# Seven more bias row sets on VectorE, and another order where the second expert layer begins

## The chip, the cores and the metric

The kernel runs on one core of a Trainium2 chip. A core has TensorE (matrix products, PE in the profile; its weight loads are PEld), VectorE (DVE), ScalarE (ACT), GpSimd (POOL) and SyncE (SP), whose queue issues nearly all transfers here. The metric is the device time of one execution in microseconds, the median of several executions; less is better.

## The reference

Three layers follow one another, all in float32, for 4 batches of 576 positions: attention with 8 heads of 64 and a learned position bias, a gated layer of width 512, and a layer that turns its input by learned angles, mixes positions, and then channels.

```python
x = (psi_rel / psi_i)[..., None]              # 576 x 576, from log1p of distances
bias = np.maximum(x @ w1 + b1, 0.0) @ w2      # 32 hidden, 8 heads
attn = softmax(q @ k.T / 8 + bias) @ v
# first expert layer: x = attn, transposed to 4 x 576 x 512
gate = 1.0 / (1.0 + np.exp(-causal_conv5(x, conv_w)))
x = (gate * (x @ w_val)) @ w_out
# second expert layer
theta = x @ w_theta
zr, zi = x * np.cos(theta), x * np.sin(theta)
y = w_tok_r @ zr + w_tok_i @ zi               # over positions
u = x + y
out = u + np.maximum(u @ w_ch, 0.0)
```

## The kernel before

**The bias stage** (the first 57 us) makes the 576 x 576 x 8 bias in 36 groups of 16 rows. For a group four tiles `h`, here called row sets, are made from the table `wpsi`: each is a maximum with a per-partition number, 304 to 577 wide. A set marked `d` is made by VectorE (line 158), one marked `a` by ScalarE (line 160). The pattern of a group is `ddda`, or `dddd` for the groups listed in `cfg["D4"]`. TensorE multiplies the sets with the second weights (line 171) into the tile `bp`, of which there are two; ScalarE scales them out of it into `ev` (line 181), and a transfer writes them to a table `scr`, from where they come back as `bias`. The order within this stage is set by the tile scheduler, which also threads the first steps of attention into it (`cfg["S0"]`).

**Attention** works in units of 128 rows and two heads: scores `s` by TensorE (line 236, two halves of 288 columns), then on VectorE line 250, which adds the bias and takes the row's extreme value (called the soft step here), the exponential on ScalarE (line 253), the normalization on GpSimd (line 265), transposes and products with the values. There are two score tiles, `s0` and `s1`, used in turn, and three tiles `ns` between VectorE and ScalarE. From the end of the bias stage on the order is the one that the code is written in.

**The products of the expert layers** are made in three matmuls each (`mm3`, lines 108 to 110): every operand is split into an upper word, a rounded copy made by ScalarE, and a lower word, the difference of both, made by GpSimd, or by VectorE where a table says `d` (`split`, lines 63 to 65). The lower word waits for the upper one.

**The second expert layer begins** in `m2`, in written order; each engine takes its instructions in that order. For batch 0 and position block t, `theta(0, t)` is 12 matmuls of 512 columns; `turns` (ScalarE, line 626) and `fold` (VectorE, line 631) reduce the angle; `trig` is three ScalarE steps (lines 637 to 639); `x(0, t)` transposes the input block on TensorE (line 645) into one of two tiles `xk_p`, so that x(0, 2) waits for the reader of x(0, 0), and so on; `z(0, t)` multiplies it on VectorE by cosine and sine (line 652, two instructions) and splits the first half of both into the upper and lower words `za`, index 0 for the cosine and 1 for the sine. Block t = 4 is a tail shared by two batches; `m2_ztail` and `m2_z8` make it. The channel weights come as 64-bit numbers, in four blocks: `L` loads one, `A` (ScalarE) and `D` (VectorE, lines 989 to 991) turn it to float32, `H` splits it, with the upper word on ScalarE (line 995) and the lower word on GpSimd (line 997). `m2_sums(0, 0)` makes the sums' words, later parts more of them (lines 666 to 680). Then `m2_tok` runs the mixing products p1, p2, p4, p6, p7, p5, p3 on TensorE; their result tiles `pp` are three, so that p6 waits until VectorE has added p1 (line 742). p1 reads the four cosine blocks of `za`, p2 the sine blocks and the tail, p4 `zb` of the sums, p6 the words that line 675 makes.

Of the kernel before, what the change touches and what calls it, by code (L numbers as in the profile page):

```python
# [14 lines left out]
PSUM = bass.MemoryType.PSUM  # L15
# [21 lines left out]

cfg = dict(

    D4=(14, 16, 18, 20, 22),  # L40

    HB=5, VB=10,

# [9 lines left out]

    TH=(0,),

    CLO='pppp', ZLO={}, SLO='p',
    XLO={(0, 4): 'p', (1, 0): 'p', (1, 1): 'p'},
)

# [53 lines left out]
class Kernel:  # L113
# [702 lines left out]
    def m2(self, top, mm, pool, T):  # L816


        tc = self.tc
        theta, turns, fold, trig, x, z = (self.m2_theta_mm, self.m2_turns, self.m2_fold, self.m2_trig, self.m2_x,  # L820
                                          self.m2_z)
        raw = self.zb_p.tile([128, KC, DM, 2], I32, tag="zb", name="raw_ch")
        blocks = [self.chan_block(raw, kc) for kc in range(KC)]

        def chan(*todo):
            for f in todo:
                blocks[int(f[1])][f[0]]()

        self.m2_fetch(1, 0)
        chan('L0', 'L1', 'A1')  # L830
        self.xk_p = pool(mm, "n_xk", 2, space=PSUM, **T)
        chan('L3', 'L2')
        self.m2_load(0)
        turns(0, 0)
        fold(0, 0)
        self.m2_fetch(0, 4)
        theta(0, 1)
        chan('A0')
        self.m2_fetch(1, 1)
        trig(0, 0)  # L840
        turns(0, 1)
        self.m2_split(0, 4)
        chan('D0')
        theta(0, 2)
        x(0, 0)
        turns(0, 2)
        self.m2_split(1, 0)
        fold(0, 1)
        trig(0, 1)
        z(0, 0)  # L850
        chan('H0')
        self.m2_split(1, 1)
        chan('A2')
        fold(0, 2)
        chan('D1')
        theta(0, 3)
        turns(0, 3)
        trig(0, 2)
        x(0, 1)
        x(0, 2)  # L860
        z(0, 1)
        x(0, 3)
        fold(0, 3)
        chan('H1', 'A3', 'D2')
        trig(0, 3)
        theta(0, 4)
        turns(0, 4)
        z(0, 2)
        fold(0, 4)
        chan('D3')  # L870
        self.m2_load(1)
        theta(1, 0)
        chan('H2')
        trig(0, 4)
        chan('H3')
        turns(1, 0)
        x(0, 4)
        z(0, 3)
        theta(1, 1)
        turns(1, 1)  # L880
        self.m2_ztail(0)
        self.m2_z8(0)
        zb = self.zb_p.tile([128, 2, 2, 4, 256], F32R, tag="zb", name="zb")
        for i, slots in enumerate((self.zh, self.zl)):
            slots += [zb[:, i, k] for k in range(2)]
        fold(1, 0)
        self.m2_sums(0, 0)
        trig(1, 0)
        fold(1, 1)
        mm.close()  # L890
        self.pp = pool(top, "n_pp", 3, space=PSUM, **T)
        self.xk_p = pool(top, "n_mm", 2, space=PSUM, **T)
        for b in range(B):
            for i, _ in enumerate(self.m2_tok(b)):
                if b == 0:
                    if i == 0:
                        self.m2_sums(0, 1)
                        self.m2_sums(0, 2)
                    if i == 1:
                        trig(1, 1)  # L900
                        self.m2_sums(0, 3)
                    if i == 2:
                        self.m2_sums(0, 4)
                    if i == 3:
                        self.m2_fetch(1, 2)
                        self.m2_fetch(1, 3)
                    if i in (5, 6):
                        self.m2_split(1, i - 3)
                elif i == 0:
                    self.m2_sums(b, 3)  # L910
                elif i == 1:
                    self.m2_sums(b, 4)
            ts = {0: (2, 3), B - 1: ()}.get(b, (0, 1, 2, 3))
            line, prev = [], None

            def turn():
                nonlocal prev
                cur = line.pop(0) if line else None
                if cur:
                    turns(*cur)  # L920
                if prev:
                    trig(*prev)
                if cur:
                    fold(*cur)
                prev = cur

            for t in ts:
                theta(b + 1, t)
                turn()
                line.append((b + 1, t))  # L930
                if b == 1 and t == 1:
                    self.m2_prep(2, 4)
            if b == 1:
                theta(2, 4)
                turn()
                line.append((2, 4))
            at = {0: 0, 1: 1, 2: 2, 4: 3}
            for i in range(2 * KC):
                n, m = i // KC, i % KC
                if b + 1 < B and i in at:  # L940
                    x(b + 1, at[i])
                if b == 1 and i == 3:
                    x(2, 4)
                if m % 2 == 0 and i:
                    out = self.pc
                self.m2_chan(b, n, m)
                if m % 2 == 0 and i:
                    new, self.pc = self.pc, out
                    self.m2_out(b, (i - 2) // KC, (i - 2) % KC)
                    self.pc = new  # L950
                if b + 1 < B and i in at:
                    z(b + 1, at[i])
                turn()
                if b == 1 and i == 3:
                    self.m2_ztail(2)
                if b + 1 < B and i == 5:
                    self.m2_sums(b + 1, 0)
                    self.m2_sums(b + 1, 1)
                if b + 1 < B and i == 6:
                    self.m2_sums(b + 1, 2)  # L960
                    self.m2_z8(b + 1)
                if b + 2 < B and i < 4:
                    self.m2_prep(b + 2, i)
            self.m2_out(b, 1, 2)
            if b + 2 < B:
                self.m2_load(b + 2)
# [8 lines left out]
    def chan_block(self, raw, kc):  # L975
# [17 lines left out]
        def parts():  # L993
            x, hi, lo = h.bitcast(F32), self.wv[0][:, kc], self.wv[1][:, kc]
            nc.scalar.activation(out=hi, in_=x, func=AF.Copy)
            eng = nc.gpsimd if cfg["CLO"][kc] == "p" else nc.vector
            eng.tensor_tensor(out=lo, in0=x, in1=hi.bitcast(F32), op=ALU.subtract)
# [79 lines left out]
    def run(self):  # L1077
# [12 lines left out]
        with ExitStack() as top:  # L1090
# [16 lines left out]
            with ExitStack() as att:  # L1107
# [12 lines left out]
                with ExitStack() as bs:  # L1120
# [19 lines left out]
                    for n in range(NG):  # L1140
                        q = "dddd" if n in cfg["D4"] else "ddda"
                        pend.append((n, q, self.bias_group(n, q, hp, pp)))
# [205 lines left out]
```

## Time and profile before

| what | us |
|---|---|
| median of 3 runs | 606.78 |
| lowest and highest | 606.68, 610.57 |
| the profiled execution | 611.05 |
| its span, first to last instruction | 609.3 |
| mean granted TensorE clock | 0.990 of full |

The profile is of one execution, whose time lies 1.75 us above its span and 4.27 us above the median. Rows of the timeline give start and length in us, engine, line, operation, `out<-in` by tile names, shapes, and how many instructions a row stands for; in brackets stands the idle time of the engine ahead of it, and what ended it.

### The profile page before, as it was taken

How to read it: one execution, taken by the hardware profiler on the slowest of the kernel's cores; microseconds unless marked ns; L12 is line 12 of the kernel's file. 1: busy time of each engine (PE TensorE's matmuls, PEld its weight loads, DVE VectorE, ACT ScalarE, POOL GpSimd, SP SyncE). 2: the span in 40 equal slices, each digit the busy share in tenths (PEclk: the TensorE clock that was granted, in tenths of full speed). 3: DMA queues.
4: the chain of work that ended last, by engine and by line, in shares of the span. 5: the costliest groups of instructions: out<-in, count | busy, mean ns of one | idle time of the engine just before them, and what ended most of it. 6: DMA issues, size and time to landing. Idle time of an engine off the chain costs nothing. (4 is left out here: it accounts for less than half of the span.)

```text
span 609.3 us, 14609 instructions
## 1 busy us (share of the span) xinstructions
PE 584.7 (96%) x5456; PEld 448.8 (74%) x5456; DVE 492.5 (81%) x1106; ACT 416.5 (68%) x912; POOL 335.9 (55%) x365
## 2 busy tenths in 40 slices
PE   6999999999999999989999999988999999999997
PEld 2334555555555555547899999868999989999997
DVE  7896899999999998777989998589757728945842
ACT  5999889888887889976468676787354267327310
POOL 0002656666665666666579776483857527643641
PEclk9999999999999999989999999979999999999999
DMA  8898799469659973203355635900213202301102
GB/s 234 239 318 259 220 230 256 152 181 240 162 149 243 249 204 100 70 21 100 98 181 177 179 113 166 332 1 0 60 50 124 81 1 75 117 1 40 40 1 77
DMA packets 51158, 84.40 MB, mean 139 GB/s; under 512 B 7168, under 2 KB 31872, under 8 KB 50576
## 3 DMA queue, kind: packets, MB, share of 16 engines
q1 hardware_dynamic: 50384, 82.53, 47.0%
q8 instruction: 43, 0.70, 0.5%
q10 hardware_dynamic: 672, 0.89, 0.4%
q14 instruction: 27, 0.22, 0.1%
q0 software_dynamic: 32, 0.07, 0.0%
HBM read 58.39 MB, written 25.07 MB: 137 GB/s over the span
## 5 line engine op out<-in xcount | busy, mean ns | idle before, releaser
L265 POOL TENSOR_SCALAR e<-e,ri 128x576 f32<-128x576 f32 x144 | 114.7, 806 | 129.6 <-DVE ri L263 81.7
L253 ACT ACTIVATE e<-ns,mx 128x576 f32<-128x576 f32 x144 | 110.9, 773 | 24.6 <-POOL e L265 12.2
L250 DVE CUSTOM_DVE_ANT_0 ns<-s,bias 128x576 f32<-128x576 f32 x128 | 94.1, 753 | 11.2 <-PE s L236 9.6
L236 PE MATMUL s<-kr,qr 64*128 64x288 f32 (+1 forms) x640 | 93.7, 424 | 0.5 <-DVE mx L250 0.5
L356 PE MATMUL o<-et,vm 128*64 128x320 f32 (+1 forms) x512 | 76.7, 422 | 1.2 <-ACT xst L376 1.2
L295 PEld LDWEIGHTS t<-idt,e 64*128 64x128 f32 x1152 | 42.9, 140 | 36.4 <-POOL e L265 19.5
L65 POOL TENSOR_TENSOR za<-zc,za 128x256 fp32r<-128x256 f32 (+1 forms) x36 | 39.8, 1124 | 51.2 <-ACT za L63 51.2
L356 PEld LDWEIGHTS o<-et,vm 128*64 128x64 f32 x512 | 31.3, 136 | 38.7 <-issue 17.4
L236 PEld LDWEIGHTS s<-kr,qr 64*128 64x128 f32 (+1 forms) x640 | 47.7, 178 | 16.0 <-DVE mx L250 4.9
L273 ACT ACTIVATE et<-t 128x512 f32<-128x512 f32 (+1 forms) x103 | 54.0, 547 | 7.9 <-PE s L308 5.6
L295 PE MATMUL t<-idt,e 64*128 64x64 f32 x1152 | 53.9, 231 | 0.4 <-ACT et L273 0.2
L525 DVE SCALAR_TENSOR_TENSOR gs<-qr,cw,gs 128x288 f32<-128x288 f32 (+4 forms) x96 | 46.1, 512 | 3.2 <-ACT gs L521 2.9
L171 PE MATMUL bp<-h,w2n 128*32 128x512 f32 (+48 forms) x648 | 43.8, 403 | 1.7 <-DVE h L158 1.0
L158 DVE TENSOR_SCALAR h<-wpsi,nbp_i 128x577 f32<-128x577 f32 (+35 forms) x113 | 41.5, 441 | 1.9 <-PE bp L171 1.6
L275 DVE COPY et<-t 128x512 f32<-128x512 f32 (+1 forms) x57 | 35.7, 625 | 7.1 <-PE t L295 6.1
L63 ACT ACTIVATE u<-x 128x288 fp32r<-128x288 f32 x32 | 12.4, 435 | 40.7 <-DVE x L742 37.3
L108 PE MATMUL pp<-wq,za 128*128 128x288 f32 x128 | 37.8, 295 | 1.8 <-DVE zc L631 1.8
L108 PE MATMUL mm<-bias,wo 128*128 128x288 f32 x128 | 38.0, 297 | 1.4 <-DVE gv L557 1.4
L108 PE MATMUL pp<-u,wv 128*128 128x288 f32 x128 | 38.8, 303 | 0.0
L109 PE MATMUL pp<-wq,za 128*128 128x288 f32 x128 | 37.9, 296 | 0.0
L109 PE MATMUL mm<-bias,wo 128*128 128x288 f32 x128 | 37.8, 295 | 0.0
L110 PE MATMUL mm<-bias,wo 128*128 128x288 f32 x128 | 37.8, 295 | 0.0
(173 smaller groups left out, 1729.3 us busy)
## 6 DMA issues: line engine op xcount, KB each, us to landing
scr<-ev SPq DMA_DIRECT2D x36, 296.0 KB, 4.3
qr<-in_q SPq DMA_DIRECT2D x32, 288.0 KB, 4.5
bias<-scr SPq DMA_DIRECT2D x32, 288.0 KB, 7.0
vm<-in_v SPq DMA_DIRECT2D x16, 320.0 KB, 5.7
kr<-in_k SPq DMA_DIRECT2D x16, 288.0 KB, 5.3
x<-x2d SPq DMA_DIRECT2D x4, 1152.0 KB, 6.3
out<-o SPq DMA_DIRECT2D x15, 288.0 KB, 2.2
xt<-x2d SPq DMA_DIRECT2D x16, 256.0 KB, 3.5
```

The lines of the kernel that those rows point to most:

```text
L108: nc.tensor.matmul(out=out, lhsT=wh, rhs=xh, start=first, stop=False)
L109: nc.tensor.matmul(out=out, lhsT=wh, rhs=xl, start=False, stop=False)
L158: nc.vector.tensor_scalar(out=dst, in0=src, scalar1=self.nbp[:, k], scalar2=None, op0=ALU.max)
L171: nc.tensor.matmul(out=ps[32 * c:32 * c + 32, n, o:o + hi - lo], lhsT=self.w2n, rhs=rhs, start=True, stop=True)
L236: nc.tensor.matmul(out=out, lhsT=w, rhs=k[r, e], start=True, stop=True)
L250: self.last_d = nc.vector.tensor_tensor_reduce(out=ns, in0=self.s4[e][:, :, :HALF], in1=bb.rearrange("p (n j) -> p n j", n=2), op0=ALU.add ...
L253: self.last_a = nc.scalar.activation(out=et[:, S * e:S * e + S], in_=ns.rearrange("p n j -> p (n j)"), func=AF.Exp, scale=-1.0, bias=mx[:, ...
L265: nc.gpsimd.tensor_scalar(out=et[:, S * e:S * e + S], in0=et[:, S * e:S * e + S], scalar1=ri[:, e:e + 1], scalar2=1.0, op0=ALU.mult, op1=A ...
L273: self.nc.scalar.activation(out=out, in_=in_, func=AF.Copy)
L295: self.nc.tensor.transpose(out=pt[h][:, 64 * kb:64 * kb + 64], in_=et[r, c:c + 128], identity=self.idt[r, r])
L356: nc.tensor.matmul(out=out, lhsT=vm[:, kb, 64 * e:64 * e + 64], rhs=rhs, start=(kb == 0), stop=(kb == 4))
L525: nc.vector.scalar_tensor_tensor(out=s[:, o:], in0=x[:, o + k:HALF + k], scalar=self.cw[:, m, k:k + 1], in1=s[:, o:], op0=ALU.mult, op1=AL ...
```

## The change

Three things change. `D4` grows from 5 groups to 12: the groups 10, 12, 24, 26, 33, 34 and 35 get their fourth row set from VectorE and no longer from ScalarE. Three lower words go from GpSimd to VectorE: that of channel block 2, and those of the cosine halves of z(0, 2) and z(0, 3). And the written order at the start of the second expert layer is another one: loads and scalings of the channel blocks stand first, with A0 ahead of the first angles; theta(0, 4) and theta(1, 0) stand ahead of x(0, 3); the folds of batch 1 stand ahead of the tail.

```diff
-    D4=(14, 16, 18, 20, 22),
+    D4=(10, 12, 14, 16, 18, 20, 22, 24, 26, 33, 34, 35),
...
-    CLO='pppp', ZLO={}, SLO='p',
+    CLO='ppdp', ZLO={(0, 2, 0): 'd', (0, 3, 0): 'd'}, SLO='p',
...
-        chan('L0', 'L1', 'A1')
-        self.xk_p = pool(mm, "n_xk", 2, space=PSUM, **T)
-        chan('L3', 'L2')
+        chan('L0', 'L1', 'A1', 'L2', 'L3', 'A0')
         self.m2_load(0)
+        theta(0, 1)
         turns(0, 0)
         fold(0, 0)
         self.m2_fetch(0, 4)
-        theta(0, 1)
-        chan('A0')
...
         trig(0, 2)
-        x(0, 1)
         x(0, 2)
         z(0, 1)
-        x(0, 3)
+        chan('A3', 'H1')
         fold(0, 3)
-        chan('H1', 'A3', 'D2')
+        self.m2_load(1)
+        chan('D2')
         trig(0, 3)
         theta(0, 4)
+        theta(1, 0)
+        x(0, 3)
         turns(0, 4)
...
+        turns(1, 1)
         fold(1, 0)
         self.m2_sums(0, 0)
+        fold(1, 1)
+        self.m2_ztail(0)
+        self.m2_z8(0)
         trig(1, 0)
-        fold(1, 1)
         mm.close()
```

On VectorE, at the end of the bias stage, the difference is this (`h_` are row sets, 544 wide in group 33 and 576 in group 35; the ISA rows are soft steps; `+` is the changed kernel):

```order
 L158 TENSOR_SCALAR h_862<-wpsi,nbp_i 128x544
+L158 TENSOR_SCALAR h_864<-wpsi,nbp_i 128x544
+L250 ISA ns,mx<-s_116,bias 128x576
+L250 ISA mx 128x1
 L158 TENSOR_SCALAR h_895<-wpsi,nbp_i 128x560
 L158 TENSOR_SCALAR h_897<-wpsi,nbp_i 128x560
 L158 TENSOR_SCALAR h_899<-wpsi,nbp_i 128x560
+L158 TENSOR_SCALAR h_901<-wpsi,nbp_i 128x560
 L158 TENSOR_SCALAR h_919<-wpsi,nbp_i 128x576
 L158 TENSOR_SCALAR h_921<-wpsi,nbp_i 128x576
 L158 TENSOR_SCALAR h_923<-wpsi,nbp_i 128x576
```

The scheduler has moved more than the table names: ahead of the last row set three soft steps stood before, and two stand now. On TensorE ten halves of scores stood singly between the groups, and now six; the others follow the last group in pairs.

On TensorE, where the second expert layer begins, the transposes (line 645) move; `x_` is the input, `xtail` the tail, and the rows between are the matmuls of the angles:

```order
 L109 MATMUL mm<-wth_82,xh 128x512
 L110 MATMUL mm<-wth_81,xl 128x512
-L645 MATMUL mm<-idt,x_6415 128x128 x12
+L645 MATMUL mm<-idt,x_6413 128x128 x8
 L108 MATMUL mm<-wth_81,xh 128x512
 L109 MATMUL mm<-wth_82,xh 128x512
@@ -2673,4 +2671,5 @@
 L109 MATMUL mm<-wth_82,xh 128x512
 L110 MATMUL mm<-wth_81,xl 128x512
+L645 MATMUL mm<-idt,x_6413 128x128 x4
 L645 MATMUL mm<-idt,xtail 128x128 x4
 L108 MATMUL mm<-wth_81,xh 128x512
```

The four transposes of x(0, 3) stood ahead of the 24 matmuls of theta(0, 4) and theta(1, 0), and now stand behind them, right ahead of the tail's.

On VectorE, in the same stretch, from the multiplies of z(0, 2) on; before:

```order
L652 TENSOR_TENSOR zc_6417<-mm,zc_6417 128x512 x2
L631 SCALAR_TENSOR_TENSOR o<-ut,mm 128x512
L989 TENSOR_SCALAR raw_ch<-raw_ch 128x512
L990 SCALAR_TENSOR_TENSOR raw_ch<-raw_ch 128x512
L991 SCALAR_TENSOR_TENSOR raw_ch<-raw_ch 128x512
L652 TENSOR_TENSOR zc_6417<-mm,zc_6417 128x512 x2
L695 TENSOR_TENSOR zt<-mm,ut 64x512
```

The changed kernel, in the same place (behind `m2` its line numbers are three lower):

```order
L652 TENSOR_TENSOR zc_6428<-mm,zc_6428 128x512 x2
L65 TENSOR_TENSOR za<-zc_6428,za 128x256
L631 SCALAR_TENSOR_TENSOR o<-ut,mm 128x512
L986 TENSOR_SCALAR raw_ch<-raw_ch 128x512
L987 SCALAR_TENSOR_TENSOR raw_ch<-raw_ch 128x512
L988 SCALAR_TENSOR_TENSOR raw_ch<-raw_ch 128x512
L994 TENSOR_TENSOR wv_977<-raw_ch,wv_976 128x512
L652 TENSOR_TENSOR zc_6428<-mm,zc_6428 128x512 x2
L65 TENSOR_TENSOR za<-zc_6428,za 128x256
L631 SCALAR_TENSOR_TENSOR zc<-zc,mm 128x512 x2
L695 TENSOR_TENSOR zt<-mm,ut 64x512
```

Three subtractions have come into VectorE's row, two of 256 columns and one of 512, and the two folds of batch 1 have come ahead of the tail's four products (line 695).

## Rows read from the trace of the kernel before

**Rows 1.** The page's part 1: busy us, share of the span, instructions

```profile
PE 584.7 (96%) x5456; PEld 448.8 (74%) x5456; DVE 492.5 (81%) x1106; ACT 416.5 (68%) x912; POOL 335.9 (55%) x365
```

**Rows 2.** Busy us by stretch: PE, PEld, DVE, ACT, POOL, clock, DMA share, GB/s

```profile
40.00:50.00 10.00, 9.87 (x122) 3.90 (x118) 9.89 (x25) 9.96 (x15) 0.00 (x0) 1.00 0.93 291
50.00:60.00 10.00, 9.51 (x150) 5.24 (x142) 4.83 (x18) 10.00 (x22) 2.94 (x4) 1.00 0.86 257
...
400.00:410.00 10.00, 9.41 (x33) 7.72 (x34) 7.82 (x10) 8.66 (x18) 8.23 (x8) 0.67 0.01 2
410.00:420.00 10.00, 8.21 (x53) 7.43 (x53) 9.74 (x13) 6.32 (x11) 6.58 (x5) 1.00 0.00 0
```

**Rows 3.** Timeline of VectorE in the bias stage

```profile
19.69 2.05 DVE L158 TENSOR_SCALAR h<-wpsi,nbp_i 128x385 f32<-128x385 f32 x6 [0.71 <-PE bp L171]
...
34.66 3.21 DVE L158 TENSOR_SCALAR h<-wpsi,nbp_i 128x400 f32<-128x400 f32 x9
...
43.63 6.49 DVE L158 TENSOR_SCALAR h<-wpsi,nbp_i 128x512 f32<-128x512 f32 x15
```

**Rows 4.** Timeline of VectorE behind the last row set

```profile
55.05 0.76 DVE L250 CUSTOM_DVE_ANT_0 ns<-s,bias 128x576 f32<-128x576 f32 x1 [3.68 <-PE s L236]
...
58.74 0.76 DVE L250 CUSTOM_DVE_ANT_0 ns<-s,bias 128x576 f32<-128x576 f32 x1
```

**Rows 5.** Timeline of TensorE at the end of the bias stage

```profile
54.94 1.23 PE L171 MATMUL bp<-h,w2n 128*32 128x512 f32 x24
56.09 1.24 PE L236 MATMUL s<-kr,qr 64*128 64x288 f32 x8
```

**Rows 6.** Timeline of ScalarE there: the last group's way out

```profile
56.63 0.83 ACT L181 ACTIVATE ev<-bp,cst_p,rpsi 128x592 f32<-128x592 f32 x1
```

**Rows 7.** Timeline of TensorE where the second expert layer begins

```profile
390.51 0.40 PE L108 MATMUL mm<-wth,xh 128*128 128x512 f32 x1
...
393.32 0.60 PE L645 MATMUL mm<-idt,x 128*128 128x128 f32 x4
...
400.58 1.09 PE L645 MATMUL mm<-idt,x 128*128 128x128 f32 x4 [3.00 <-DVE zc L652]
...
417.75 0.40 PE L108 MATMUL pp<-wq,za 128*128 128x288 f32 x1 [1.79 <-DVE zc L631]
...
425.83 0.29 PE L108 MATMUL pp<-wq,zb 128*128 128x288 f32 x1
```

**Rows 8.** Timeline of VectorE there

```profile
391.31 0.69 DVE L991 SCALAR_TENSOR_TENSOR raw_ch<-raw_ch 128x512 int32<-128x512 int32 x1
...
404.14 1.28 DVE L652 TENSOR_TENSOR zc<-mm,zc 128x512 f32<-128x512 f32 x2
407.50 0.69 DVE L631 SCALAR_TENSOR_TENSOR o<-ut,mm 128x512 f32<-128x512 f32 x1 [2.08 <-ACT ut L626]
...
410.05 1.69 DVE L991 SCALAR_TENSOR_TENSOR raw_ch<-raw_ch 128x512 int32<-128x512 int32 x1
411.66 1.28 DVE L652 TENSOR_TENSOR zc<-mm,zc 128x512 f32<-128x512 f32 x2
...
415.69 0.69 DVE L65 TENSOR_TENSOR zl<-zt,zh 128x512 fp32r<-128x512 f32 x1
416.41 1.29 DVE L631 SCALAR_TENSOR_TENSOR zc<-zc,mm 128x512 f32<-128x512 f32 x2
...
422.48 0.75 DVE L742 TENSOR_TENSOR x<-pp,x 128x576 f32<-128x576 f32 x1
```

**Rows 9.** Timeline of ScalarE there

```profile
387.53 1.32 ACT L571 ACTIVATE xo<-mm 128x288 f32<-128x288 f32 x4 [1.45 <-DMA x2d<-xo]
...
404.82 0.71 ACT L639 ACTIVATE zc<-zc,hpi 128x512 f32<-128x512 f32 x1
406.77 0.69 ACT L626 ACTIVATE ut<-mm,magic 128x512 f32<-128x512 f32 x1 [1.24 <-PE mm L110]
```

**Rows 10.** Timeline of GpSimd there

```profile
409.43 1.76 POOL L997 TENSOR_TENSOR wv<-raw_ch,wv 128x512 fp32r<-128x512 f32 x1
```

More of the change, by code (lines that the diff above doesn't have):

```diff
@@ L836, in m2 @@
         self.m2_fetch(0, 4)
-        theta(0, 1)
-        chan('A0')
-        self.m2_fetch(1, 1)
+        self.xk_p = pool(mm, "n_xk", 2, space=PSUM, **T)
         trig(0, 0)
@@ L842, in m2 @@
         self.m2_split(0, 4)
+        self.m2_fetch(1, 1)
         chan('D0')
+        self.m2_split(1, 0)
         theta(0, 2)
         x(0, 0)
+        fold(0, 1)
         turns(0, 2)
-        self.m2_split(1, 0)
-        fold(0, 1)
         trig(0, 1)
         z(0, 0)
-        chan('H0')
-        self.m2_split(1, 1)
[L853 to L857, printed above, removed]
+        fold(0, 2)
+        chan('D1', 'H0')
+        theta(0, 3)
+        chan('A2')
+        turns(0, 3)
+        self.m2_split(1, 1)
+        x(0, 1)
         trig(0, 2)
-        x(0, 1)
         x(0, 2)
         z(0, 1)
-        x(0, 3)
+        chan('A3', 'H1')
         fold(0, 3)
-        chan('H1', 'A3', 'D2')
+        self.m2_load(1)
+        chan('D2')
         trig(0, 3)
         theta(0, 4)
+        theta(1, 0)
+        x(0, 3)
         turns(0, 4)
@@ L869, in m2 @@
         fold(0, 4)
[L870 to L873, printed above, removed]
+        chan('D3', 'H2')
         trig(0, 4)
+        x(0, 4)
         chan('H3')
         turns(1, 0)
-        x(0, 4)
+        theta(1, 1)
         z(0, 3)
[L879 to L882, printed above, removed]
         zb = self.zb_p.tile([128, 2, 2, 4, 256], F32R, tag="zb", name="zb")
```

## The prediction

> **What bounds the kernel now.** I read the page first, then the busy time by stretch, then the timelines of the two places that the change touches. TensorE is busy for 96% of the span [rows 1], so from 60 us on nearly every microsecond taken out of a stall moves the end by as much, and a faster VectorE, ScalarE or GpSimd is worth only the TensorE time that waited for it. The reader is to see two places where TensorE does wait, or is not its own master. In the bias stage TensorE, VectorE and ScalarE are all full: 9.87, 9.89 and 9.96 of 10 us between 40 and 50 [rows 2]. Then ScalarE alone is full (10.00 of 10) and VectorE half idle (4.83) [rows 2]. At the start of the second expert layer TensorE stands still for 3.00 us ahead of x(0, 3), and for 1.79 us ahead of p2 [rows 7]; behind the first of these stalls the granted clock is 0.67 over ten microseconds, part of them at 1.2 GHz, against 1.00 (2.4 GHz) in the stretch with the second [rows 2]. The first wait is for the multiplies of z(0, 1), which free the tile; the second for the folds of batch 1, which stand behind the tail on VectorE, until 417.70 [rows 8].
>
> **The bias stage, from both sides.** Seven row sets leave ScalarE and come to VectorE. On VectorE one costs 3.21 / 9 = 0.36 us near 400 columns and 6.49 / 15 = 0.43 near 512 to 576 [rows 3]. Groups 10 and 12 fall in a time when VectorE waits for TensorE anyway (0.71 us ahead of 19.69 is the longest of these waits) [rows 3] and cost nothing; if that idle time were gone they would cost 0.7. Groups 24, 26, 33, 34 and 35 stand in the full stretch: 2 x 0.36 + 3 x 0.43 = 2.0 us. Against that, one soft step of 0.76 us [rows 4] has moved behind the last row set. The last set, which ended at 43.63 + 6.49 = 50.1 [rows 3], so ends at 50.1 + 2.0 - 0.8 = 51.3. What does that give? Before, the last group left TensorE at 56.1 [rows 5] and ScalarE at 57.5 [rows 6]: ScalarE's chain ended last, and it gets shorter. If TensorE followed the last set by its 1.23 us [rows 5], the last group would be through at 52.6, 3.5 us sooner. But five soft steps, not four, then follow on VectorE, with the scores of three of them after the group; before, the first of four started at 55.05 and the last at 58.74 [rows 4], so five take (58.74 - 55.05) / 3 x 4 = 4.9 us from the first start to the last. The first now starts at about 52.6 and a half (the scores' pair), 53.1, and the last at 58.0, against 58.74: 0.7 us gained. The bounds: soft steps spaced at their bare 0.76 give 53.1 + 3.0 = 56.1, 2.6 gained; TensorE, which was itself 99% busy [rows 2] and has to feed the groups at the pace it had, may bring the last group only 1 us later than I say, and then 0.3 is lost. TensorE is helped there by the four halves of scores that no longer stand singly among the groups: eight in a row take 1.24 [rows 5]. I take -0.8, near the worked value, with -2.6 and +0.3 as ends. That transfers take it back I don't expect: their share is 0.93 and 0.86 here [rows 2], and the waits in these rows are for engines.
>
> **The start of the second expert layer.** A0 moves into a hole: ScalarE waited 1.45 us ahead of 387.53 [rows 9], which covers it, and costs 0.6 were the hole gone. The loads change places on SyncE's queue (L2 before L3), which nobody waits for: both land long before A2. x(0, 3) moves behind theta(0, 4) and theta(1, 0), 24 matmuls; TensorE no longer stalls at 397.58. It then has 5.6 us of angles to run at the full clock (12 took 393.32 - 390.51 = 2.8 [rows 7]) and reaches x(0, 3) at 403.2, when its tile is long free, and the tail's transposes at 403.6. Those wait for the multiplies of z(0, 2), 404.14 + 1.28 = 405.4 [rows 8]: a new stall of 1.8 us. theta(1, 1) ends at 408.7, 4 us sooner than before, and p1 can begin.
>
> But p1 needs the cosine words of z(0, 3), p2 the folds, p6 the add of p1: all VectorE. So I follow VectorE from 404.14, where nothing upstream has changed for it. Before, the stretch to the end of the add of p1 (422.48 + 0.75 = 423.2) holds 2.08 us of idle time, ahead of the fold of block 4; ScalarE waited 1.24 us for TensorE then [rows 8, 9]. Now theta(0, 4) is done at 400.4, ScalarE is free of trig(0, 3) at 405.5 [rows 9] and makes the turns at once, and the idle time is gone. New in the row are: a wait for the upper word of za, which stands behind these turns on ScalarE, 0.5; its subtraction, 0.4 (a little over half of the 0.69 for 512 columns [rows 8]); one of 512 columns, 0.69; a second wait, 0.45, and a second subtraction, 0.4. The three steps of D3 took from 408.1 to 411.66, 3.6 us, beside GpSimd [rows 8, 10]; the last of them takes 0.69 undisturbed, and three at most so take 2.1, rather 1.8. GpSimd has lost two of the subtractions that lay there, so I take 2.7, between the ends. Sum from 404.14: multiplies 1.28, wait 0.5, subtraction 0.4, fold 0.6, D3 2.7, block 2's word 0.65, then what ran from 411.66 to 423.2, 11.5, in another order and with 0.85 more: 404.1 + 6.1 + 12.4 = 422.6 to 422.7. The add of p1 ends 0.6 us sooner, and p6, for which TensorE was late before (425.83 [rows 7]), now follows it at 422.8. TensorE itself is through p1 at 413.2, p2 at 417.7, p4 at 421.7 (p2 and p4 together took 425.83 - 417.75 = 8.1 [rows 7]): less late than VectorE. Gain at p6: 3.0 us; with D3 at 1.8 it is 3.9, with 3.6 it is 2.1. Behind p6 TensorE hardly waits, and the gain stays.
>
> One part of this is uncertain by the run: a clock of 0.67 over ten microseconds [rows 2] is 6.6 us at half rate, which cost TensorE some 3 us before, and the timed runs, 4.3 us under the profiled one, may not have it. Without it VectorE's idle time would have been 1.3 shorter, and the gain 1.7. I take 2.3, with ends of 1.0 and 3.9.
>
> **A rule against it.** D3's last step took 1.69 us beside GpSimd's subtraction at 409.43, and the same step 0.69 with GpSimd idle at 391.31 [rows 8, 10]. Three more two-input subtractions on VectorE can each meet such a neighbour, at +1.0. The Trainium skill ("SBUF — State Buffer", Who interferes with whom) says that a VectorE instruction with two SBUF inputs contends with a GpSimd one that reads SBUF, and that the second to start blocks until the first is done; the trace agrees, since a step of 0.69 begun at GpSimd's end, 411.19, would have ended at 411.88, and this one did at 411.74 [rows 8, 10].
>
> **The rivals.** *Crowded VectorE*: all three moved subtractions are delayed by 1.0 and D3 stays at 3.6. p6 then starts at 422.8 + 3.0 + 0.9 = 426.7, 0.9 later than before; with the bias stage's -0.8 the kernel stands at about 606.9. For it speaks D3; against it, that GpSimd has less to do in this stretch than before. 15%. *ScalarE was the whole bound of the bias stage*: it gives its 2.6, and the second layer 2.3 to 3.9: 600.3 to 601.9. For it: ScalarE full from 50 to 60 [rows 2]; against: the soft steps that have moved behind. 14%. *The row sets do nothing*, since three engines are full there and the scheduler's new order eats what ScalarE saves: 606.8 - 2.3 = 604.5, inside the forecast's own range. *Slower*: the new stall of 1.8 us ahead of the tail's transposes, with p1's wait for its last words behind it, brings the low clock back, and it lasts. A stall of 3.00 us brought it for 6.6 us, one of 1.79 did not [rows 2, 7]. If it lasted 6.6 us from 405 on, p1 would end near 414.6 and p4 near 422.7, no later than VectorE. It decides from about 13 us on: 20 us at half rate would put p6 at 429.5, 3.7 late, and the kernel at 606.8 - 0.8 + 3.7 = 609.7. 4%.
>
> **How the numbers follow.** Forecast: 606.8 - 0.8 - 2.3 = 603.7, with 601.9 to 606.1 as its own range; 67%. The range for 8 in 10 takes in part of both neighbours: 601.2 to 606.8. One per cent, about what a measurement of this kernel tells from no change, is 600.7 and 612.8. Faster than that: the lower half of the ScalarE rival and the outermost of the forecast, 10%. Slower than that: only mechanisms that I don't see, or a clock that stays low for long, 3%. The rest, 87%.
>
> **What would show it.** Right: the last soft step of the first eight starts near 58; no stall ahead of x(0, 3), a stall of 1.5 to 2.5 us ahead of the tail's transposes; p1 before 409.5 less the shift of the bias stage; p6 released by VectorE's add of p1 (line 739 there), 3 us sooner. Wrong: ScalarE's last `ev` and the soft steps both 2.5 us sooner; a clock under 0.8 between 400 and 420; VectorE's subtractions of line 65 at 1 us or more.

## The result and the profile after

| | us |
|---|---|
| median of 7 runs of the changed kernel | 603.40 |
| lowest and highest | 602.87, 606.40 |
| the kernel before beside it, median of 7 | 609.16 (606.68 to 610.57) |
| ratio | 0.9917, 95% interval 0.989 to 0.9945 |
| the profiled execution, its span | 602.87, 601.1 |

The kernel is faster by 5.1 us (3.4 to 6.7), where 3.1 was forecast. The time itself, 603.4, is where the forecast put it (603.7), but partly because two errors cancel: the three runs from which the forecast started gave 606.78, and more runs of the kernel before gave 609 to 610.

The page's part 1 of the changed kernel, then the same stretches as [rows 2]:

```profile
PE 578.6 (96%) x5456; PEld 444.7 (74%) x5456; DVE 492.3 (82%) x1116; ACT 413.2 (69%) x905; POOL 333.4 (55%) x362
```

```profile
40.00:50.00 10.00, 9.96 (x130) 4.05 (x134) 9.90 (x26) 9.66 (x16) 0.00 (x0) 1.00 0.98 309
50.00:60.00 10.00, 9.03 (x134) 4.86 (x126) 7.12 (x24) 8.41 (x18) 4.34 (x6) 1.00 0.94 281
...
400.00:410.00 10.00, 7.79 (x48) 6.58 (x46) 8.87 (x16) 8.79 (x17) 5.74 (x6) 1.00 0.01 2
410.00:420.00 10.00, 9.99 (x75) 9.75 (x75) 9.63 (x14) 6.91 (x12) 1.86 (x1) 1.00 0.00 0
```

No engine's work has changed much: VectorE is busy for 492.3 us against 492.5 [rows 1]. What has gone is waiting, and a stretch at 1.2 GHz: the granted clock is 1.00 from 400 to 410, against 0.67 [rows 2].

The end of the bias stage in the changed kernel. VectorE:

```profile
7.64 33.77 DVE L158 TENSOR_SCALAR h<-wpsi,nbp_i 128x545 f32<-128x545 f32 x96
...
46.92 3.49 DVE L158 TENSOR_SCALAR h<-wpsi,nbp_i 128x560 f32<-128x560 f32 x8
...
53.79 0.76 DVE L250 CUSTOM_DVE_ANT_0 ns<-s,bias 128x576 f32<-128x576 f32 x1 [2.43 <-PE s L236]
...
57.26 0.76 DVE L250 CUSTOM_DVE_ANT_0 ns<-s,bias 128x576 f32<-128x576 f32 x1
```

TensorE's last products of row sets, 112 in one piece:

```profile
47.43 5.63 PE L171 MATMUL bp<-h,w2n 128*32 128x511 f32 x112
```

and ScalarE's last evictions there:

```profile
52.43 1.60 ACT L181 ACTIVATE ev<-bp,cst_p,rpsi 128x592 f32<-128x592 f32 x2
54.59 0.77 ACT L253 ACTIVATE e<-ns,mx 128x576 f32<-128x576 f32 x1 [0.56 <-DVE mx L250]
```

VectorE's 96 row sets from 7.64 on run in one piece: the waits for TensorE of [rows 3] are gone. The last set ends at 50.41, only 0.3 later than before, though VectorE makes seven more. ScalarE is through the last group at 54.0 instead of 57.5 [rows 6], and the last soft step of the first eight stands at 57.26 instead of 58.74 [rows 4]. Of these 1.5 us, 0.2 is there already at ScalarE's third eviction (12.70 against 12.93), ahead of every group that changes.

The start of the second expert layer on VectorE, to be read against [rows 8]:

```profile
400.47 1.28 DVE L652 TENSOR_TENSOR zc<-mm,zc 128x512 f32<-128x512 f32 x2
402.79 0.43 DVE L65 TENSOR_TENSOR za<-zc,za 128x256 fp32r<-128x256 f32 x1 [1.04 <-ACT za L63]
403.13 0.68 DVE L631 SCALAR_TENSOR_TENSOR o<-ut,mm 128x512 f32<-128x512 f32 x1
403.73 0.42 DVE L986 TENSOR_SCALAR raw_ch<-raw_ch 128x512 int32<-128x512 int32 x1
404.19 0.69 DVE L987 SCALAR_TENSOR_TENSOR raw_ch<-raw_ch 128x512 int32<-128x512 int32 x1
404.92 0.69 DVE L988 SCALAR_TENSOR_TENSOR raw_ch<-raw_ch 128x512 int32<-128x512 int32 x1
405.52 0.68 DVE L994 TENSOR_TENSOR wv<-raw_ch,wv 128x512 fp32r<-128x512 f32 x1
406.13 1.28 DVE L652 TENSOR_TENSOR zc<-mm,zc 128x512 f32<-128x512 f32 x2
407.33 0.73 DVE L65 TENSOR_TENSOR za<-zc,za 128x256 fp32r<-128x256 f32 x1
407.98 1.27 DVE L631 SCALAR_TENSOR_TENSOR zc<-zc,mm 128x512 f32<-128x512 f32 x2
...
412.62 1.22 DVE L666 TENSOR_TENSOR zc<-zc 128x1024 f32<-128x1024 f32 x1
...
416.73 0.76 DVE L742 TENSOR_TENSOR x<-pp,x 128x576 f32<-128x576 f32 x1
```

and TensorE's three waits there, with p4's and p6's first products (against [rows 7]):

```profile
401.85 0.63 PE L645 MATMUL mm<-idt,xtail 128*128 128x128 f32 x4 [1.62 <-issue]
...
408.11 0.40 PE L110 MATMUL pp<-wq,za 128*128 128x288 f32 x1 [0.19 <-DVE za L65]
...
409.31 0.40 PE L108 MATMUL pp<-wq,za 128*128 128x288 f32 x1 [0.41 <-DVE zc L631]
...
413.39 0.30 PE L108 MATMUL pp<-wq,zb 128*128 128x288 f32 x1
...
417.54 0.40 PE L108 MATMUL pp<-wq,zb 128*128 128x288 f32 x1
```

The profile puts the first of these waits down to "issue"; it ends 0.1 us after the multiplies of z(0, 2), whose end (400.47 + 1.28) frees the tile that the transposes write. The folds of batch 1 end at 409.25, and p2 follows at 409.31. Before, they ended at 417.70 [rows 8]. p6 starts at 417.54, right behind the add of p1 (416.73 + 0.76 = 417.49), against 425.83 [rows 7]. Of these 8.29 us, 3.42 were there when the layer's angles began (375.10 against 378.52): 1.5 by the end of the bias stage, 1.5 from a stretch in attention that was at 1.2 GHz only in the profile before, 0.4 not traced. So 4.9 us belong to the start of the second layer in this pair of profiles. The kernel ends 8.2 us sooner.

### The profile page after: what moved, and what is told of

It is laid out like the page before. It is cut to its first block, busy times and chain, and to the rows that moved or that the text cites. A ratio compares the mean times of both kernels' runs of the same rounds, so it can differ in the third digit from the quotient of the medians.

```text
span 601.1 us, 14613 instructions
## 1 busy us (share of the span) xinstructions
PE 578.6 (96%) x5456; PEld 444.7 (74%) x5456; DVE 492.3 (82%) x1116; ACT 413.2 (69%) x905; POOL 333.4 (55%) x362
## 4 chain that ended last, share of the span: by engine, by line
PE 64%; DVE 14%; ACT 12%; DMA 4%; issue 4%; POOL 1%; DVEq 0%; ACTq 0%; SPq 0%
PE pp L108 9%; PE pp L109 9%; PE pp L110 9%; PE o L356 9%; PE s L236 9%; PE bp L171 6%; PE t L295 5%; ACT e L253 3%; DVE ns L250 3%; DMA qr<-x1d 2%; PE mm L108 2%; PE mm L110 2%; PE mm L109 2%; DVE et L275 1%; DVE raw L525 1%
## 5 line engine op out<-in xcount | busy, mean ns | idle before, releaser
L236 PE MATMUL s<-kr,qr 64*128 64x288 f32 (+1 forms) x640 | 92.2, 424 | 0.7 <-DVE mx L250 0.7
L65 POOL TENSOR_TENSOR za<-zc,za 128x256 fp32r<-128x256 f32 (+1 forms) x34 | 38.3, 1144 | 49.9 <-ACT za L63 49.7
L158 DVE TENSOR_SCALAR h<-wpsi,nbp_i 128x577 f32<-128x577 f32 (+35 forms) x120 | 43.7, 439 | 0.5
L108 PE MATMUL mm<-bias,wo 128*128 128x288 f32 x128 | 37.9, 296 | 1.5 <-DVE gv L557 1.5
L108 PE MATMUL pp<-wq,za 128*128 128x288 f32 x128 | 37.8, 296 | 0.4 <-DVE zc L631 0.4
L110 PE MATMUL pp<-wq,za 128*128 128x288 f32 x128 | 37.8, 295 | 0.2 <-DVE za L65 0.2
L109 PE MATMUL pp<-wq,za 128*128 128x288 f32 x128 | 37.9, 296 | 0.0
L110 PE MATMUL mm<-bias,wo 128*128 128x288 f32 x128 | 37.8, 295 | 0.0
```

Source lines behind the costliest of these rows:

```text
L108: nc.tensor.matmul(out=out, lhsT=wh, rhs=xh, start=first, stop=False)
L109: nc.tensor.matmul(out=out, lhsT=wh, rhs=xl, start=False, stop=False)
L110: nc.tensor.matmul(out=out, lhsT=wl, rhs=xh, start=False, stop=last)
L236: nc.tensor.matmul(out=out, lhsT=w, rhs=k[r, e], start=True, stop=True)
```

## The experiments

Each kernel's ratio is against runs of the kernel before on the same chip, which were 610 us in the median. "From the angles" counts in a profile from the first product of theta.

**The kernel before again.** No edit.

> The kernel before, unchanged, profiled again. The first profile had two episodes at 1.2 GHz, behind the stalls of 1.51 us at 263.83 and of 3.00 us at 397.58. Theory (the episodes are chance, the stalls are not): both stalls are there again, at least one of the episodes is missing, and the span is 1.5 to 4 us shorter than 609.3 for it; the ratio to itself is 1.000 within 0.3%. Rival (each such stall always brings the low clock): both episodes come again, and the span is 609.3 within 0.5 us.

Measured: 610.58 us, ratio 1.0008 (0.9991 to 1.0026); the profiled execution took 611.25, its clock was 0.993. Both stalls are there (1.51 and 2.85 us), and so are both stretches at 1.2 GHz, the second half as long as in the first profile. That is the rival's outcome, here. So the clock's part is no accident of one profile: the kernel before runs so, and the 606.78 of its first three runs was its low end. In all 76 further runs of the kernel before, the granted clock is 0.990 to 0.997; in six of the first seven of the changed kernel it is 0.999 or 1.000. p6 stands 45.97 us from the angles, 47.31 in the first profile: 1.3 us is about how far the clock moves it.

**Each half alone.** The kernel before with the new `D4`:

```diff
-    D4=(14, 16, 18, 20, 22),
+    D4=(10, 12, 14, 16, 18, 20, 22, 24, 26, 33, 34, 35),
```

> The kernel before with the twelve groups of row sets on VectorE, and nothing else of the change. Theory (the two parts add up): what TensorE does at 100 us comes 1.5 us sooner, as in the changed kernel, and the time is 1.5 us under before, ratio 0.9975. Rival (the gain at 100 us is lost again in the layers behind, which are held by something else): ratio 1.000.

and the changed kernel with the old `D4` (the same diff, the other way):

> The changed kernel with the five old groups of row sets: only the second layer's order and the three lower words are changed. Theory (the order takes away TensorE's stall of 3.00 us, and VectorE no longer waits at the start of the layer): p6 starts 3.0 to 4.5 us sooner against the start of the layer's angles than before, and the time is 2.5 to 4.5 us under before, ratio 0.9925 to 0.996. Rival (most of it was the low clock in the one profile of before): under 1.5 us, ratio over 0.9975.

Measured: 0.997 (0.9955 to 0.9986), 1.8 us, for the row sets; 0.994 (0.9918 to 0.9962), 3.7 us, for the second layer. Their product is the whole change's 0.991. In the second, p6 stands 42.54 us from the angles (42.44 in the changed kernel, 45.97 and 47.31 before). Both theories hold, and the two halves add up. The gain of the row sets isn't lost in attention: counted from ScalarE's third eviction, the eighth soft step comes 1.2 us sooner than before and the 101st still 1.2.

**The words back on GpSimd.**

```diff
-    CLO='ppdp', ZLO={(0, 2, 0): 'd', (0, 3, 0): 'd'}, SLO='p',
+    CLO='pppp', ZLO={}, SLO='p',
```

> The changed kernel with the three lower words back on GpSimd. Theory (the order does the work, the words little): VectorE's row is 1.8 us shorter, but p1's last cosine words of z(0, 3) come from GpSimd, behind the block's word of 1.3 us; p1 waits 0.5 to 1.5 us longer and p6 starts within 0.7 us of the changed kernel; ratio to before 0.991 to 0.994. Rival 1 (the words on VectorE are a cost): p6 1 us or more sooner, ratio under 0.990. Rival 2 (the words are what lets p1 and p2 go): p6 1.5 us or more later, ratio over 0.994.

Measured: 0.9916 (0.9898 to 0.9934), p6 43.75 us from the angles, 1.3 later than in the changed kernel. VectorE's block 3 in this kernel:

```profile
404.10 0.77 DVE L986 TENSOR_SCALAR raw_ch<-raw_ch 128x512 int32<-128x512 int32 x1
404.91 1.11 DVE L987 SCALAR_TENSOR_TENSOR raw_ch<-raw_ch 128x512 int32<-128x512 int32 x1
406.05 1.68 DVE L988 SCALAR_TENSOR_TENSOR raw_ch<-raw_ch 128x512 int32<-128x512 int32 x1
```

and GpSimd beside it:

```profile
403.85 1.62 POOL L65 TENSOR_TENSOR za<-zc,za 128x256 fp32r<-128x256 f32 x2 [0.41 <-ACT za L63]
405.43 1.75 POOL L994 TENSOR_TENSOR wv<-raw_ch,wv 128x512 fp32r<-128x512 f32 x1
```

From the first of these steps to the next instruction on VectorE it is 3.6 us, in the changed kernel 1.8. The three words cost VectorE 0.43 + 0.68 + 0.73 = 1.84 us there, and give 1.8 back in block 3; p1 no longer waits 0.66 us for a word from GpSimd. Of the 1.3 us, 0.7 is there already at the layer's first fold (11.3 us from the angles against 10.6), ahead of everything that differs; from the multiplies of z(0, 2) to p6 it is 17.7 us against 17.1. So by the profile the words are worth 0.6 us, within the theory's 0.7, and the times can't tell that from nothing.

**The changed kernel again**, beside the next three. No edit.

> The changed kernel, unchanged, beside the same runs of the kernel before as the next three. Theory (the two parts add: 0.997 for the row sets alone, 0.994 for the second layer alone): ratio 0.991, within 0.002, no stretch under 2.4 GHz at the start of the second layer, stall ahead of the tail's transposes 1.6 us. Rival (the words on VectorE bring something that the run with the words on GpSimd at 0.9916 did not have): under 0.989, and the difference of 1.3 us that p6 showed between those two profiles is seen again in the time.

Measured: 604.65 us, 0.991 (0.9891 to 0.9928); stall ahead of the tail 1.44 us, p6 42.25 us from the angles. Theory right.

**x(0, 3) back in its old place.**

```diff
         z(0, 1)
+        x(0, 3)
         chan('A3', 'H1')
...
         theta(1, 0)
-        x(0, 3)
```

> The changed kernel with x(0, 3) alone put back ahead of theta(0, 4) and theta(1, 0), so that TensorE waits there for the multiplies of z(0, 1). Theory (TensorE's own wait is the smaller part: VectorE sets p2 and p6): a stall of 2.5 to 3 us stands ahead of x(0, 3) again and the one of 1.6 us ahead of the tail's transposes goes; p1 starts 1 to 2 us later than in the changed kernel, p6 0.5 to 1.5 later, plus some 1 us where the clock falls to 1.2 GHz behind the stall; ratio 0.992 to 0.995. Rival 1 (the move of x(0, 3) is the whole of the second layer's gain): ratio 0.996 to 0.998. Rival 2 (VectorE alone decides): 0.991, as the changed kernel.

Measured: 0.9918 (0.9897 to 0.9938), p6 43.56 us from the angles. The stall is back, 2.49 us, and behind it the clock is 0.75 between 395 and 400; the stalls ahead of the tail, p1's last words and p2 are gone. p1 starts 2.4 to 2.6 us later, more than the 1 to 2 expected, and p6 1.1 to 1.3, less than the 1.5 to 2.5 expected where the clock falls. p6 begins 1.16 us behind the add of p1 here: TensorE sets it, and not VectorE, against the theory. The time can't be told from the changed kernel's. So the move of x(0, 3) is worth 1.1 to 1.3 us of p6's place, the smaller part of the second layer's gain.

**The old stall filled with useless work.** The kernel before, with theta(0, 4) done twice into the same tile:

```diff
         z(0, 1)
+        theta(0, 4)
         x(0, 3)
```

> The kernel before, with the twelve products of theta(0, 4) done twice: a first time, for nothing, ahead of x(0, 3), where TensorE stands still for 2.9 to 3.0 us, and again at their old place. The order of everything else is as before. Theory (the clock has a price of its own): TensorE is busy over the old stall, the clock stays at 2.4 GHz from 390 to 410, and the profiled p6 comes 1 to 1.7 us sooner, since a stretch of 3.4 us at half rate costs 1.7; ratio 0.997 to 0.9985. Rival 1 (TensorE at half rate there only waits less for VectorE): clock at 2.4 GHz, p6 unchanged, ratio 1.000. Rival 2 (the clock doesn't come from that stall): 1.2 GHz is seen again and the ratio is 1.000.

Measured: 1.0007 (0.9989 to 1.0025). TensorE's waits, and the busy time by stretch:

```profile
412.86 0.40 PE L110 MATMUL pp<-wq,za 128*128 128x288 f32 x1 [0.50 <-POOL za L65]
416.03 0.61 PE L108 MATMUL pp<-wq,za 128*128 128x288 f32 x1 [2.38 <-DVE zc L633]
```

```profile
400.00:404.00 4.00, 4.00 (x21) 3.17 (x20) 3.93 (x6) 3.94 (x9) 4.00 (x4) 1.00 0.01 4
...
416.00:420.00 4.00, 3.97 (x16) 3.98 (x17) 3.73 (x4) 2.55 (x6) 0.88 (x1) 0.50 0.00 0
420.00:424.00 4.00, 4.00 (x26) 4.00 (x26) 3.95 (x7) 3.27 (x6) 0.00 (x0) 0.78 0.00 0
```

The clock is at 2.4 GHz over the old stall, and p1 starts 3.1 us sooner than in the first profile (409.55). But p2 waits for the same folds, and the low clock has moved behind that wait: from p2 to p6 TensorE takes 10.6 us instead of 8.1. The folds end 37.6 us from the angles, against 39.2 and 37.9 in the two profiles of the kernel before. So the filled stall brought p2 0.3 to 1.6 us, and 1.2 GHz between p2 and p6, where TensorE waits for nobody, took 2.5. None of the three expectations fits whole: the time is rival 1's and 2's, but the clock does have a price of its own, and the useless work only moved the low clock. The runs agree: the two of twelve with a granted clock of 0.999 took 607.46 and 609.06, the six at 0.994 took 610.73 to 611.82.

**Channel block 2 behind z(0, 2).** `chan('D2')` moved behind `z(0, 2)`, and `ZLO={(0, 3, 0): 'd'}`.

> The changed kernel with VectorE's three steps of channel block 2 (3.2 us) moved from ahead of the multiplies of z(0, 2) to behind them, and the lower word of z(0, 2) back on GpSimd. Theory (VectorE's row as a whole sets p2 and p6): the stall of 1.6 us ahead of the tail's transposes goes, but comes back ahead of p1's last words and of p2; p2 and p6 start 0.3 to 1.2 us sooner, for the 1.04 us that VectorE no longer waits ahead of that word; ratio 0.989 to 0.9905. Rival (the stall was TensorE's own): p6 1.6 us sooner, ratio 0.988 or under. Third: the word from GpSimd comes too late for p1, and nothing is gained, 0.991.

Measured: 0.9926 (0.9909 to 0.9942). The stall ahead of the tail goes, and a stall of 1.80 us stands ahead of p1's last cosine words instead, with 1.2 GHz behind it. The folds end 34.4 us from the angles, 34.15 in the changed kernel: VectorE's row is no shorter, since it now waits 0.98 ahead of z(0, 2). p6 stands 44.04 us from the angles, 1.6 later than in the changed kernel. Nothing gained, the third expectation's result, but not for the word from GpSimd, which was early.

**The folds first, alone.** The kernel before, with one move:

```diff
         turns(1, 1)
+        fold(1, 0)
+        fold(1, 1)
         self.m2_ztail(0)
...
-        fold(1, 0)
         self.m2_sums(0, 0)
         trig(1, 0)
-        fold(1, 1)
```

> The kernel before with one move alone: the folds (1, 0) and (1, 1) written ahead of the tail's products and z8 on VectorE, where they stood behind them. Theory (p2 waits for these folds, and what stands ahead of them on VectorE is the cost): the folds end 3.5 us sooner, near 414.2 in the time of the first profile, the stall of 1.79 us ahead of p2 goes, and p6 starts 1.8 us sooner against the end of the last row of the attention; ratio 0.996 to 0.998. Rival 1 (the add of p1, which the move doesn't touch, sets p6): p6 unchanged, 1.000. Rival 2 (the tail's words, now later, hold up p2's own last products): under 0.7 us gained, 0.999.

Measured: 0.9976 (0.9962 to 0.9991), 1.5 us: the theory's size, near the low end. The folds end at 413.26, the wait ahead of p2 is gone, and p6 stands 45.65 us from the angles, 0.3 to 1.7 sooner than before. New waits stand behind it:

```profile
419.00 0.40 PE L110 MATMUL pp<-wq,zb 128*128 128x288 f32 x1 [0.49 <-POOL zb L65]
423.74 0.40 PE L108 MATMUL pp<-wq,zb 128*128 128x288 f32 x1 [0.76 <-DVE x L742]
```

The second is the add of p1, late because line 666 took 3.41 us here (last section); so p6 waits for that add again, as in rival 1, only sooner.

**The tail ahead of the folds**, in the changed kernel: `m2_ztail(0)` and `m2_z8(0)` back ahead of `fold(1, 0)`.

> The changed kernel with the tail's products and z8 put back ahead of the folds (1, 0) and (1, 1). Theory: the folds end 3.5 us later, TensorE stands still ahead of p2 for some 3.8 us instead of 0.41, p6 comes 3 to 3.5 us later than in the changed kernel, and with the low clock that a stall of this length can bring another 1 to 2: ratio 0.996 to 0.999, most of the second layer's gain gone. Rival (the gain comes from VectorE's row as a whole, which is as long as before): p6 within 1 us, ratio 0.991 to 0.993.

Measured: 0.9989 (0.9971 to 1.0006), although the new row sets, worth 1.8 us, are in it. TensorE's wait ahead of p2, and the clock behind it:

```profile
412.95 0.61 PE L108 MATMUL pp<-wq,za 128*128 128x288 f32 x1 [3.98 <-DVE zc L631]
```

```profile
412.00:416.00 4.00, 3.05 (x13) 3.05 (x13) 3.90 (x5) 2.16 (x4) 1.80 (x1) 0.58 0.00 0
```

p6 stands 47.24 us from the angles, 4.8 later than in the changed kernel: 3.6 from the longer wait, 1.2 behind p2, where the clock is low. Everything else of the second layer's new order is still there, and p6 stands where it stood before (45.97 and 47.31).

**Written on.** The changed kernel with `chan('D0', 'D1')` together ahead of the second fold, block 3 ahead of the fold of block 4, `trig(0, 4)` behind the turns of batch 1, and `ZLO={(0, 3, 0): 'd'}`.

> The changed kernel, written on: the steps of channel block 1 on VectorE (2.8 us) go into its idle 2.04 us ahead of the second fold, block 3's ahead of the fold of block 4, ScalarE makes the turns of batch 1 before the last sines, and the lower word of z(0, 2) is GpSimd's. Theory (VectorE and ScalarE set the stalls of 1.6 and 0.4 us that are left): both go, p1 starts 1.5 us sooner and p6 1 to 1.8 sooner against the start of the angles than in the changed kernel, the ratio is 0.988 to 0.990. Rival 1 (ScalarE, full from 390 to 410, takes it back: the tail waits for the last sines): p2 sooner but p6 unchanged, 0.991. Rival 2 (GpSimd, which now works beside block 1's steps, lengthens them): 0.9905 or more, the steps of L987 and L988 over 1.1 us.

Measured: 0.9917 (0.9896 to 0.9938). Nearest is rival 1, and worse: the tail waits for the last sines (line 695 starts at 411.07 after 1.11 us of waiting), p2 stops for 1.34 us ahead of its own last words, and p6 comes 1.4 us later from the angles. No version here has a lower ratio than the changed kernel's 0.991.

**Without groups 10 and 12**: `D4=(14, 16, 18, 20, 22, 24, 26, 33, 34, 35)`.

> The changed kernel without groups 10 and 12 among the row sets on VectorE (ten groups instead of twelve). Theory (ScalarE's chain sets the pace of the whole bias stage, early too): ScalarE's evictions from the tenth on come 0.7 us later than in the changed kernel, counted from the second, the last soft step of the first eight 0.5 to 0.8 us later; ratio 0.992. Rival (these two groups fall in idle time and neither cost nor give): the evictions of the last groups and the soft steps as in the changed kernel within 0.2 us; ratio 0.991.

Measured: 0.9927 (0.9901 to 0.9953). VectorE's waits are back:

```profile
20.42 2.06 DVE L158 TENSOR_SCALAR h<-wpsi,nbp_i 128x385 f32<-128x385 f32 x6 [0.71 <-PE bp L171]
...
24.48 3.21 DVE L158 TENSOR_SCALAR h<-wpsi,nbp_i 128x337 f32<-128x337 f32 x10 [0.47 <-PE bp L171]
```

Counted from ScalarE's third eviction, which leaves out how the stage begins, the last soft step of the first eight comes after 45.68 us; 44.56 and 44.55 in the two profiles of the changed kernel, 45.81 before. That is 1.1 later than in the changed kernel, where 0.5 to 0.8 was expected. The eleventh eviction comes 0.9 later. So, at the soft step, nearly all of the bias stage's gain hangs on these two groups, with what the scheduler makes of them: it also placed the soft steps otherwise (the first at 34.72, not 41.32). The time alone (0.9927 against 0.991) is too coarse to say so, and it holds something else: the stall ahead of the tail was 1.99 us here, with 3.4 us at 1.2 GHz behind it, and p6 stands 43.10 us from the angles, 0.7 later.

## Why the prediction was right in its sign and short in its size

**The base.** It took 606.8, the median of three, and held it open whether the timed runs have the low clock. They have it: the later medians are 610.58 and 610.36. Both sums were made against the base, so the time came out right with a gain 2 us too small. That is luck.

**The bias stage, -0.8.** The ends, -2.6 and +0.3, hold what was measured, 1.3 to 1.5 at the soft step and 1.8 in the time. Three terms were off, and not all the same way. *Groups 10 and 12 cost nothing* was true and not the whole of it: VectorE's waits there were taken as free room, but they were waits for TensorE, whose weight loads waited for ScalarE to empty `bp` and to make the fourth sets. In the kernel before, from 3 to 50 us (us in total, times, longest):

```profile
PEld bp L171 <- ACT ev L181: 9.8, 19, 0.9
...
PEld bp L171 <- ACT h L160: 1.5, 4, 0.4
```

Taking those sets from ScalarE took 1.6 us of waits out of VectorE's row (0.71 + 0.20 + 0.47 + 0.24 in the trace before), so the last set ended at 50.41 and not at 51.3. But *TensorE follows the last set by its 1.23 us* failed: TensorE worked without a pause from 47.43 to 53.06, ended 2.6 us behind the last set, and so the first of the five soft steps stood at 53.79 and not at 53.1. And the five soft steps were given the spacing of before, 1.23 us, as if it were their own. It was the mean of 1.96, 0.96 and 0.77, and the first of these holds a wait for scores that TensorE made behind the last group's 24 products [rows 5]:

```profile
57.01 0.76 DVE L250 CUSTOM_DVE_ANT_0 ns<-s,bias 128x576 f32<-128x576 f32 x1 [1.20 <-PE s L236]
```

In the changed kernel these scores follow the last group together, and four spacings took 57.26 - 53.79 = 3.47, 1.4 less than forecast. With the first soft step 0.7 late that makes the 0.7 by which the gain at the soft step was too small.

**The second layer, -2.3.** Measured 3.7 in the time (2.3 to 5.0), 3.4 to 5.1 in profiles. The mechanism came out as it was named: VectorE's row decides, TensorE is no longer late from p2 on, and p6 follows the add of p1 (line 742 in both kernels; 739 was a slip), where before it began 2.6 us behind it. The lead is narrow: p4's last product starts at 417.23, and products before it follow one another by 0.13, so TensorE waited for that add by some 0.2 us. Which part of the new order takes TensorE's lateness away, the sum doesn't say: the folds ahead of 3.5 us of tail stand in it as *in another order*, without a price. They are the largest piece: put back, they cost 4.8 us of p6's place; alone they give 1.5 us. The rest needs VectorE's row to be shorter too, which the move alone doesn't have.

The allowance for the clock, 2.3 between 3.0 with the low clock of the first profile and 1.7 without, was no mistake in kind: against the first profile p6 gained 4.9 us, against the second, with half as long a stretch at 1.2 GHz, 3.5. What made all of these too small are terms of VectorE's row: the first wait was 1.04 us, not 0.5; the second wait wasn't there, not 0.45, and the word behind it took 0.65, not 0.4; D3 took 1.8, the low end, not 2.7; line 666 took 1.22 and not 2.08, which was in no term. From the multiplies of z(0, 2) to the end of the add of p1 it is 417.49 - 400.47 = 17.0 us, against 18.5 forecast. Before it was 19.1, but 17.9 in the second profile and 17.7 with the row sets alone, so 1.2 to 1.4 of these 2.1 us are missing already where the stretch at 1.2 GHz behind the old stall is half as long. The stall ahead of the tail, 1.8 forecast, was 1.62.

**The rule and the crowded VectorE.** The rule of the Trainium skill ("SBUF — State Buffer", Who interferes with whom) was weighed as a danger for three more subtractions on VectorE. The measured 0.43, 0.68 and 0.73 show little of it, 0.3 us in the third. It worked the other way: with its words gone, GpSimd was no longer beside block 3's steps. The rival had the right mechanism and looked at the new instructions only, not at the ones that got rid of a neighbour.

**The clock as a rival** (the new stall brings it): no stretch under 1.00 followed the stall of 1.62 us, nor those of 1.72 (the second layer alone) and 1.44 (the changed kernel again); one did follow the 1.99 in the kernel without groups 10 and 12. Nor is the whole gain one of the clock: with x(0, 3) early and with block 2 moved, most runs have a granted clock of 0.996 or 0.997, as the best runs of the kernel before have, and their ratios are 0.9918 and 0.9926.

## What to carry to other kernels

Where TensorE waits twice in a row, ask of each wait whether the next one would swallow its removal: here filling the longer stall, 3.00 us, changed the time by nothing, since p2 still waited behind it and the low clock then stood behind p2, while taking away the cause of the shorter one gave 1.5 us alone. Price the order of a vector engine's row by the one instruction in it that somebody waits for, not by the row's end. And a wait on an engine is not free room until it is known that the same change doesn't remove it.

## What the runs showed of the hardware

**A VectorE step with two inputs in SBUF that met a GpSimd subtraction ended a fixed time after it.** Line 666 (128x1024) took three lengths, by when GpSimd's 128x1024 subtraction was over: 1.21 or 1.22 us where it had ended before, 2.08 in the kernel before and 2.07 with the tail first, and this with the folds first:

```profile
416.62 3.41 DVE L666 TENSOR_TENSOR zc<-zc 128x1024 f32<-128x1024 f32 x1
```

```profile
416.24 2.71 POOL L65 TENSOR_TENSOR zb<-zc,zb 128x1024 fp32r<-128x1024 f32 x1 [2.67 <-ACT zb L63]
```

418.95 + 1.08 = 420.03 is where it ended. In the other two it ended 1.08 behind GpSimd as well (418.61 and 419.69; 413.80 and 414.88). It did so in all six profiles in which the two met. That the later one waits for the whole of the earlier one agrees with the rule cited above, and it makes such a step's price a matter of when it starts. The tail's products (line 695), with one input in PSUM, took 0.67 to 0.70 in every kernel, also while GpSimd worked.

**Which stalls bring 1.2 GHz is not settled by their length alone.** In attention near 264 TensorE stands still for 1.51 or 1.52 us in thirteen of the fourteen profiles; the clock fell behind it in two of these (both of the kernel before), and also in the fourteenth (the changed kernel again), where the stall is 2.00. At the start of the second layer it fell with all seven stalls of 2.38 to 3.98 us, not with one of 2.31, and with three of the five of 1.79 to 1.99. What else decides was not tried.
